# Tokens of the small blocks gathered and transposed ahead, and the second transposes' copies split, in an attention and mixture-of-experts kernel

## The chip, the cores and the metric

The kernel runs on one core of one Trainium2 chip. The metric is device time in microseconds (us) for one execution of the whole program, and lower is better. The core has a matmul engine (PE, with its weight loads shown as PEld), VectorE (DVE), ScalarE (ACT), GpSimd (POOL) and SyncE (SP, which here only issues DMAs). Each engine works through its own instructions in order and waits for others by semaphores.

## The reference: what is computed

Block-local attention with pooled far keys makes x of 3072 tokens by 512, and a two-level router sends each token to one of 16 experts. Cut to what matters here:

```python
x = attn_out.transpose(0, 2, 1, 3).reshape(B * S, H * D)      # 3072 x 512
for g in range(4):                                             # group of the token
    for e in range(4):                                         # expert within the group
        mask_e = ...                                           # tokens routed to expert (g, e)
        h = np.maximum(xg[mask_e] @ w1[g, e], 0.0)             # 512 -> 1024
        ye = h @ w2[g, e]                                      # 1024 -> 512
        out[tok_idx] = combined[:, None] * ye
```

How many tokens each expert gets depends on the data; the kernel counts them on the chip.

## The kernel before

The first part of the program is the attention (to about 175 us), with the router's arithmetic woven in. Then come the experts. Each expert's tokens are cut into blocks of 128: "first" blocks (four, of the largest expert), "pairs" (two blocks of one expert, 256 tokens), "ones" (single blocks left over) and "smalls" (a remainder of at most SM = 32 tokens, which would waste a whole block). The numbers of pairs, ones and smalls are read into registers, and `rest` (L1296) runs the blocks under `If`s: for i in 0 to BESIDE - 1 = 3 pair i and then small i, after that the other pairs, then the ones. With this data there are 8 pairs, 3 smalls and 3 ones, so smalls 0, 1 and 2 run behind pairs 0, 1 and 2.

A pair (`pair`, L1158) computes `stage1_2` (x times w1, with both split into a high and a low float32r part) and then twice `stage2` (h times w2), one for each half of 128 tokens. `stage2` is a generator: it hands back control after every 6 of its 24 matmuls, and there `pair` puts one part of `split_w`, which makes the next pair's high and low w1 (`w1h` by a cast on ACT, then `w1l` by a subtraction on DVE, 4 parts in all, in half 0 only). Each pair also starts the loads of the next pair's weights and, for i from 1 to 3, of small i's weights, on SP's queue.

A small (`small`, L1230) uses plain float32 and packs the 32 tokens four times into the 128 columns: the gather `gather_small` (L1226) brings one 128-column chunk of a token to each partition. Its steps follow each other on PE:

- a transpose of the gathered tokens into the PSUM tile `tp` (bank "tr" 2), and a copy of it by DVE into `xTs`;
- 16 matmul calls with w1 (stage 1), a Relu by ACT into `hs`;
- two transposes of `hs` into `tp`, a single DVE copy of both into `hTs`;
- 32 matmul calls with w2 (stage 2, chunks c = 0 to 7 in order), a scaled copy by ACT, and a scatter on POOL.

The gather of small i + 1 is issued in small i, behind its first transpose; that of small 0 in `first` (L1272). All of a small's buffers (`xgs`, `ys`, `xTs`, `hs`, `hTs`) are 128-column slices of one tile that the router no longer needs, so the profile shows them all as `eq_unit`. The operations made through `self.T` and `self.V` are all shown with line L123, a helper's. `bank` returns a fixed PSUM tile of one bank once the first blocks are done.

Of the kernel before, what the change touches and what calls it, by code (L numbers as in the profile page):

```python
# [20 lines left out]
P = 128  # L21
# [18 lines left out]
SM = 32  # L40
# [3 lines left out]
BESIDE = 4  # L44
SMALL = 2 * NPAIR + NONE
SLOTS = SMALL + NSM
KC, FC = DM // P, FF // P
# [28 lines left out]
class Banks:  # L76


    def __init__(self, tiles):
        self.tiles, self.n = tiles, 0  # L80
# [888 lines left out]
class Experts:  # L969
# [12 lines left out]
    def tiles(self, pool, early):  # L982
        def ring(name, shape, dt, n):
            return [pool.tile(shape, dt, name=f"{name}{j}") for j in range(n)]

        def pair(name, shape, n):
            return list(zip(ring(name + "h", shape, F32R, n), ring(name + "l", shape, F32R, n)))
        if early:
            self.w2r["first"] = self.w2r[1] = pool.tile([P, FC, DM], F32, name="w2r1")
            self.w1s = pair("w1", [P, KC, FC, P], 1)[0]  # L990

            self.xg1 = ring("xg", [P, DM], F32, 2)

            self.xT2 = ring("xT", [P, 2, KC, 2, P], F32R, 1)
            self.hT2 = pair("hT", [P, FC, 2 * P], 1)[0]

            o = self.router.ohr
            self.xT2.append(o[:, 0:16].rearrange("p (m c a) t -> p m c a t", m=2, a=2))
            self.xg2 = [None, o[:, 16:24].bitcast(F32).rearrange("p (a c) t -> p a (c t)", a=2)]
        else:  # L1000
            self.w1r[0], self.w1r[1] = ring("w1r", [P, KC, FF], F32, 2)
            self.w2r[0] = pool.tile([P, FC, DM], F32, name="w2r0")
            self.w2s = pair("w2", [P, FC, DM], 1)[0]
            self.xg2[0] = pool.tile([P, 2, DM], F32, name="xd")
            self.xT1 = ring("xs", [P, KC, P], F32, 2)
            self.y = ring("y", [P, DM], F32, 2)
            self.ny = 0
            eq = self.router.eq = pool.tile([P, NT, SLOTS], F32, name="eq_unit")
            parts = [eq.rearrange("p t s -> p (t s)")[:, P * i:P * i + P] for i in range(9)]
            self.xgs, self.ys, self.xTs = parts[0:2], parts[2:4], parts[4]  # L1010
            self.hs = eq.rearrange("p t s -> p (t s)")[:, 5 * P:7 * P]
            self.hTs = eq.rearrange("p t s -> p (t s)")[:, 7 * P:9 * P].rearrange("p (c r) -> p c r", r=SM)

# [144 lines left out]
    def pair(self, i):  # L1158

        row, nxt = ("unit", i), ("unit", i + 1)

        self.gather2(i + 2)
        self.load_w(("next", i + 1), 0)
        if 0 < i < BESIDE:
            self.load_w(("small", i), 0, self.n_small > i)
        for k, _ in enumerate(self.stage1_2(i)):
            if k % 2 == 0:
                self.split_w(row, 1, [k // 2])  # L1170
            if k == XT_AT:
                self.x_t2(i + 1)
        self.load_w(("next", i + 1), 1)
        if 0 < i < BESIDE:
            self.load_w(("small", i), 1, self.n_small > i)
        if i == 0:
            self.x_t_one(0)
        for half in range(2):
            hs = slice(half * P, half * P + P)
            for part, _ in enumerate(self.stage2([t[:, :, hs] for t in self.hT2], row, half, half)):  # L1180
                if half == 0 and i + 1 < NPAIR:
                    self.split_w(nxt, 0, [part])


    def gather_one(self, i):
# [39 lines left out]

    def gather_small(self, i):  # L1226
        if i < NSM:
            self.gather(("small", i), self.xgs[i % 2])

    def small(self, i):  # L1230

        nc, row = self.nc, ("small", i)
        w1, w2 = self.raw(row, 0), self.raw(row, 1)
        groups = [slice(SM * g, SM * g + SM) for g in range(P // SM)]
        tp = self.bank("tr", 2)
        self.T.transpose(out=tp[:, 0:P], in_=self.xgs[i % 2], identity=self.ident)
        self.gather_small(i + 1)
        self.V.tensor_copy(out=self.xTs, in_=tp[:, 0:P])
        bank = self.bank("lg", 0)
        hp, yp = bank[:, 0:2 * P], bank[:, 2 * P:3 * P]  # L1240

        def load(which):
            if i + 1 < NSM:
                more = self.n_small > i + 1
                self.load_w(("small", i + 1), which, more if i >= BESIDE - 1 else more * (self.n_pairs <= i + 1))
        for c in range(KC):
            for g, rows in enumerate(groups):
                self.T.matmul(out=hp[rows], lhsT=self.xTs[:, SM * c:SM * c + SM], rhs=w1[:, c, 2 * P * g:2 * P * g + 2 * P],
                              start=(c == 0), stop=(c == KC - 1), skip_group_check=True)
        nc.scalar.activation(out=self.hs, in_=hp, func=AF.Relu)  # L1250
        load(0)
        for m in range(2):
            self.T.transpose(out=tp[:, P * m + P:P * m + 2 * P], in_=self.hs[:, P * m:P * m + P], identity=self.ident)
        self.V.tensor_copy(out=self.hTs.rearrange("p (g m) r -> p m g r", m=2),
                           in_=tp[:, P:3 * P].rearrange("p (m g r) -> p m g r", m=2, r=SM))
        for c in range(FC):
            for g, rows in enumerate(groups):
                self.T.matmul(out=yp[rows], lhsT=self.hTs[:, c], rhs=w2[:, c, P * g:P * g + P],
                              start=(c == 0), stop=(c == FC - 1), skip_group_check=True)
        load(1)  # L1260
        y = self.ys[i % 2]
        nc.scalar.activation(out=y, in_=yp, func=AF.Copy, scale=self.tabs["small", "weight"][:, i:i + 1])
        self.put(y, row)
# [8 lines left out]
    def first(self):  # L1272
        for i in range(0, NE, 2):
            for k, _ in enumerate(self.stage1_2(0)):
                if i == 0 and k >= 4:
                    self.split_w(("first", 0), 1, [k - 4], what="h")
                yield
            if i + 2 < NE:
                self.x_t1()
                yield  # L1280
            for half in range(2):
                s2 = self.stage2([t[:, :, half * P:half * P + P] for t in self.hT2], ("first", i + half),
                                 late=None if i + half else lambda c: self.split_w(("first", 0), 1, [c], what="l"))
                if i + half < NE - 1:
                    yield from s2
        yield "units"
        for part, _ in enumerate(s2):
            self.split_w(("unit", 0), 0, [part])
            if part == 0:
                self.x_t2(0)  # L1290
                for i in range(2):
                    self.gather_one(i)
                self.gather_small(0)
        self.fixed = True

    def rest(self):  # L1296
# [49 lines left out]
def block_attention_then_moe(tc, q, k, v, w_group, w_expert, w1, w2, out):  # L1346
    with ExitStack() as st:
# [15 lines left out]
        def hook(n, need, space):  # L1363

            if not ex.w1r and n >= W1_AT and (router.ready & 1 or n == last - 4):
                need(1)
                ex.w1r["first"] = space
                ex.load_w(("first", 0), 0)
            if n == last - 4:
                ex.tiles(st.enter_context(tc.tile_pool(name="m_w", bufs=1, side="right")), True)  # L1370
            if n == last - GATHER_AT:
                need(2)
                ex.gather1(0)
            if n == last - W2_AT:

                ex.load_w(("first", 0), 1, queue=tc.nc.scalar)
            if n == last - X_AT:
                ex.x_t1()
                if NE > 2:
                    ex.gather1(2)  # L1380
            for part in range(4):
                if n == last + SPLIT_AT[part]:
                    ex.split_w(("first", 0), 0, [part])
            for _ in range(FIRST.get(n - last, 0)):
                next(first)
# [63 lines left out]
```

## Time and profile before

| | us |
|---|---|
| median of 3 runs | 541.56 |
| lowest and highest of them | 539.62, 542.04 |
| the profiled execution | 543.24 |
| its span, first to last instruction | 541.5 |

The profile comes from one execution. A row of the timeline gives the start from the beginning of the span, the duration, engine, line, operation, what is written and read, the count of merged instructions, and in brackets the idle time of the engine before it and what ended that. `PEclk` in the rows by windows is the granted clock of PE as a share: 1.00 is 2.4 GHz and 0.50 is 1.2 GHz.

### The profile page before, as it was taken

The numbers are of one execution on the slowest core, as the hardware profiler recorded it, in microseconds if no ns is written. First come the engines' busy times: TensorE is split into PE (matmuls) and PEld (weight loads), VectorE is DVE, ScalarE is ACT, GpSimd is POOL, SyncE is SP. The second block draws the span as 40 slices with busy tenths as digits, with TensorE's granted clock in tenths as the row PEclk, the third lists the DMA queues.
The fourth block names the chain that finished last, engine by engine and source line by source line (L and its number), as shares of the span: only waits on it lengthen the run. The fifth ranks groups of instructions, "written<-read, shape, count | busy, mean of one in ns | idle before, by whom it ended". The sixth has DMA issues, their size and how long they took to land. (4 is left out here: it accounts for less than half of the span.)

```text
span 541.5 us, 13168 instructions
## 1 busy us (share of the span) xinstructions
PE 492.9 (91%) x4873; PEld 412.7 (76%) x4873; DVE 312.2 (58%) x1001; ACT 289.0 (53%) x561; POOL 151.2 (28%) x166
## 2 busy tenths in 40 slices
PE   6798888898989899989979899999999999999991
PEld 3576667677777787979859697889898998977770
DVE  6666788788865869756706354465474836540000
ACT  5688888899976551116615354445464644541110
POOL 6553543353443201054021130402021121210110
PEclk9899999999987999988989999999999999999997
DMA  9668965796681620299719879667666657636950
GB/s 225 141 152 160 210 175 143 176 209 149 143 274 41 234 79 21 77 385 399 289 37 374 321 292 391 217 207 259 231 198 232 213 197 245 244 105 242 305 194 21
DMA packets 80837, 111.15 MB, mean 205 GB/s; under 512 B 42732, under 2 KB 51310, under 8 KB 77936
## 3 DMA queue, kind: packets, MB, share of 16 engines
q1 hardware_dynamic: 74992, 93.31, 55.5%
q0 software_dynamic: 4704, 14.69, 7.4%
q10 hardware_dynamic: 1056, 2.10, 1.1%
q8 instruction: 44, 0.72, 0.6%
q14 instruction: 41, 0.34, 0.2%
HBM read 118.27 MB, written 13.04 MB: 242 GB/s over the span
## 5 line engine op out<-in xcount | busy, mean ns | idle before, releaser
L123 PE MATMUL ps_s<-xT,w1h 128*128 128x256 f32 x448 | 84.2, 285 | 0.4 <-PEq L1328 0.4
L123 DVE TENSOR_TENSOR w2l<-w2r,w2h 128x1024 fp32r<-128x1024 f32 x40 | 48.8, 1226 | 53.8 <-ACT w2h L1064 51.9
L1116 POOL DMA_INDIRECT out_dram<-y,t_unit_scatter x21 | 22.1, 1050 | 193.7 <-ACT y L1110 106.3
L123 PEld LDWEIGHTS ps_s<-xT,w1h 128*128 128x128 f32 x448 | 70.7, 191 | 1.6 <-issue 1.3
L123 PE MATMUL ps_s<-xT,w1l 128*128 128x256 f32 x224 | 63.3, 283 | 0.0
L821 ACT ACTIVATE pr<-ss,nm 128x120 f32<-128x120 f32 x192 | 60.1, 388 | 3.9 <-DVE nm L812 3.5
L1154 ACT ACTIVATE hTh<-ps_s 128x512 fp32r<-128x512 f32 x44 | 26.3, 598 | 55.6 <-PE ps_s L123 35.1
L750 POOL TENSOR_TENSOR va<-vr,share 24x512 f32<-24x512 f32 x48 | 49.6, 1058 | 14.4 <-DMA vr<-vs 11.0
L123 DVE TENSOR_TENSOR w1l<-w1r,w1h 128x1024 fp32r<-128x1024 f32 x40 | 46.5, 1222 | 3.0 <-ACT w1h L1064 3.0
L123 PE MATMUL ps_s<-ohr,w1h 128*128 128x256 f32 x256 | 48.1, 286 | 0.0
L123 DVE SCALAR_TENSOR_TENSOR hTl<-ps_s,hTh 128x512 fp32r<-128x512 f32 x44 | 30.4, 690 | 27.7 <-ACT hTh L1154 27.7
L812 DVE CUSTOM_DVE_ANT_0 ss<-mask,ps_s 128x120 f32<-128x120 f32 x192 | 42.0, 274 | 3.0 <-ACT pr L821 2.3
L123 PEld LDWEIGHTS ps_s<-xT,w1l 128*128 128x128 f32 x224 | 42.8, 191 | 0.2
L1064 ACT CAST w2h<-w2r 128x1024 fp32r<-128x1024 f32 x40 | 41.5, 1042 | 0.8 <-issue 0.4
L123 PEld LDWEIGHTS ps_s<-ohr,w1h 128*128 128x128 f32 x256 | 40.5, 192 | 0.7 <-issue 0.6
L829 ACT COPY ptS<-ps_tr 121x512 f32<-121x512 f32 x48 | 28.1, 586 | 20.3 <-PE ps_tr L123 8.2
L1064 ACT CAST w1h<-w1r 128x1024 fp32r<-128x1024 f32 x40 | 38.9, 1046 | 0.0
L123 PE MATMUL ps_s<-kw,qt 64*64 64x120 f32 x768 | 34.1, 284 | 4.6 <-DVE kw L757 2.3
L790 POOL COPY kw<-kf 128x1152 f32<-128x1152 f32 x15 | 17.3, 1154 | 73.5 <-DVE kf L781 39.4
L777 ACT ACTIVATE qt<-ps_tr 64x384 f32<-64x384 f32 x64 | 33.3, 521 | 5.9 <-PE ps_tr L123 4.7
L123 PE MATMUL ps_s<-ohr,w1l 128*128 128x256 f32 x128 | 36.3, 284 | 0.0
L123 PE MATMUL ps_s<-w2h,hTh 128*128 128x512 f32 x88 | 35.7, 406 | 0.0
(255 smaller groups left out, 1050.2 us busy)
## 6 DMA issues: line engine op xcount, KB each, us to landing
w1r<-in_moe_w_dram SPq DMA_DIRECT2D x40, 1024.0 KB
w2r<-in_moe_w_dram SPq DMA_DIRECT2D x40, 1024.0 KB
va<-in_v_dram SPq DMA_DIRECT2D x32, 240.0 KB
kn<-in_k_dram SPq DMA_DIRECT2D x16, 384.0 KB
qn<-in_q_dram SPq DMA_DIRECT2D x16, 384.0 KB
x_dram<-xt SPq DMA_DIRECT2D x12, 512.0 KB
w_first<-in_moe_w_dram SPq DMA_DIRECT2D x2, 1024.0 KB
w2r<-in_moe_w_dram ACTq DMA_DIRECT2D x2, 1024.0 KB
```

The costliest lines, as they stand in the source:

```text
L123: return f(*args, **kw)
L750: nc.gpsimd.tensor_tensor(out=va_ring[idx % NVA][KW:NC, t:t + n, :, 0:D], in0=vr[KW:NC].broadcast_to([NBLK, n, 2, D]), in1=by(share, KW, N ...
L777: nc.scalar.activation(out=by_run(qb, h)[:, j], in_=tv, func=AF.Copy, scale=-1.0 / 8.0)
L790: (nc.gpsimd if idx else V).tensor_copy(out=kw[:, :, 0:KW], in_=tiles)
L812: V.tensor_tensor_reduce(out=ss[:, u], in0=mask[:, 1 if t == 0 else 2 if t == NQT - 2 else 0], in1=sp[h][:, j], scale=1.0, scalar=3.4e38, ...
L821: nc.scalar.activation(out=pr[:, i, 0:NC], in_=sp[:, i], func=AF.Exp, bias=nm[:, i:i + 1], scale=-1.0)
L829: nc.scalar.copy(out=ptS.rearrange("p a c -> p (a c)"), in_=pt[0:NR])
L1064: self.nc.scalar.copy(out=h, in_=src)
L1116: self.nc.gpsimd.indirect_dma_start(out=out, out_offset=bass.IndirectOffsetOnAxis(ap=self.tabs[name, "scatter"][:, col:col + 1], axis=0), ...
L1154: nc.scalar.activation(out=th[:, js], in_=hp, func=AF.Relu)
```

## The change

Three things are changed. First, the tokens of smalls 0 to 3 are all gathered in `first`, one behind the other on POOL, into four buffers (two of them in slices that later hold `hs` and `hTs`). Second, their transposes and DVE copies (`x_t_small`) move from the smalls into pair 0: two of them behind the third part (18 matmuls) of `stage2` for half 0, and two at the same place for half 1; all four go through bank "tr" 2. Smalls 4 and later keep the old way. Third, behind the Relu of a small, the two transposes get a copy each: the first's is made by ACT, the second's by DVE, and stage 2 takes the chunks in the order 0, 2, 4, 6, 1, 3, 5, 7, so that its first half needs ACT's copy only.

```diff
-            parts = [eq.rearrange("p t s -> p (t s)")[:, P * i:P * i + P] for i in range(9)]
-            self.xgs, self.ys, self.xTs = parts[0:2], parts[2:4], parts[4]
+            parts = [eq.rearrange("p t s -> p (t s)")[:, P * i:P * i + P] for i in range(8 + BESIDE)]
+            self.xgs, self.ys, self.xTs = parts[0:2] + parts[5:8:2], parts[2:4], parts[4:5] + parts[9:8 + BESIDE]
...
                 if half == 0 and i + 1 < NPAIR:
                     self.split_w(nxt, 0, [part])
+                if i == 0 and part == 2:
+                    for j in range(2 * half, min(2 * half + 2, BESIDE)):
+                        self.x_t_small(j)
...
+    def x_t_small(self, i):
+        tp = self.bank("tr", 2)[:, i % 2 * P:i % 2 * P + P]
+        self.T.transpose(out=tp, in_=self.x_in(i), identity=self.ident)
+        self.V.tensor_copy(out=self.x_small(i), in_=tp)
...
     def small(self, i):
+        if i >= BESIDE:
+            self.x_t_small(i)
+        if i >= BESIDE - 1:
+            self.gather_small(i + 1)
+        xT = self.x_small(i)
         tp = self.bank("tr", 2)
-        self.T.transpose(out=tp[:, 0:P], in_=self.xgs[i % 2], identity=self.ident)
-        self.gather_small(i + 1)
-        self.V.tensor_copy(out=self.xTs, in_=tp[:, 0:P])
...
-        for m in range(2):
-            self.T.transpose(out=tp[:, P * m + P:P * m + 2 * P], in_=self.hs[:, P * m:P * m + P], identity=self.ident)
-        self.V.tensor_copy(out=self.hTs.rearrange("p (g m) r -> p m g r", m=2),
-                           in_=tp[:, P:3 * P].rearrange("p (m g r) -> p m g r", m=2, r=SM))
-        for c in range(FC):
+        hTs = self.hTs.rearrange("p (g m) r -> p m g r", m=2)
+        for m, copy in enumerate((nc.scalar.copy, self.V.tensor_copy)):
+            tm = tp[:, P * m + P:P * m + 2 * P]
+            self.T.transpose(out=tm, in_=self.hs[:, P * m:P * m + P], identity=self.ident)
+            copy(out=hTs[:, m], in_=tm.rearrange("p (g r) -> p g r", r=SM))
+        order = [*range(0, FC, 2), *range(1, FC, 2)]
+        for c in order:
...
-                self.gather_small(0)
+                for i in range(BESIDE):
+                    self.gather_small(i)
```

## Rows read from the trace of the kernel before

**Rows 1.** The page's first section: busy us (share of span) x instructions, by engine.

```profile
PE 492.9 (91%) x4873; PEld 412.7 (76%) x4873; DVE 312.2 (58%) x1001; ACT 289.0 (53%) x561; POOL 151.2 (28%) x166
```

**Rows 2.** Windows: length; busy of PE, PEld, DVE, ACT, POOL; PEclk, DMA share, GB/s.

```profile
284.30:306.60 22.30, 22.30 (x144) 20.25 (x144) 13.14 (x14) 10.74 (x14) 3.58 (x3) 1.00 1.01 380
...
309.50:311.00 1.50, 0.44 (x3) 0.20 (x3) 0.42 (x1) 0.38 (x1) 1.20 (x2) 1.00 0.04 14
```

**Rows 3.** Timeline of small 1, all engines (small 2 repeats it within 0.01 us).

```profile
306.85 0.27 PE L123 MATMUL ps_tr<-ident,eq_unit 128*128 128x128 f32 x1
...
307.16 0.29 DVE L123 COPY eq_unit<-ps_tr 128x128 f32<-128x128 f32 x1 [5.06 <-PE ps_tr L123]
...
307.55 1.93 PE L123 MATMUL ps_lg<-w1r,eq_unit 128*32 128x256 f32 x32 [0.43 <-issue]
...
309.61 0.38 ACT L1250 ACTIVATE eq_unit<-ps_lg 128x256 f32<-128x256 f32 x1 [1.82 <-PE ps_lg L123]
310.04 0.44 PE L123 MATMUL ps_tr<-ident,eq_unit 128*128 128x128 f32 x2 [0.56 <-ACT eq_unit L1250]
310.52 0.42 DVE L123 COPY eq_unit<-ps_tr 128x256 f32<-128x256 f32 x1 [3.06 <-PE ps_tr L123]
...
311.00 2.10 PE L123 MATMUL ps_lg<-w2r,eq_unit 128*32 128x128 f32 x64 [0.52 <-DVE eq_unit L123]
```

**Rows 4.** Timeline of small 0: the same first step on PE.

```profile
274.39 0.27 PE L123 MATMUL ps_tr<-ident,eq_unit 128*128 128x128 f32 x1
275.05 1.94 PE L123 MATMUL ps_lg<-w1r,eq_unit 128*32 128x256 f32 x32 [0.38 <-DVE eq_unit L123]
```

**Rows 5.** Groups with shapes kept apart: 128x128 moves out of PSUM, busy, mean ns.

```profile
L1262 ACT ACTIVATE eq_unit<-ps_lg,t_small_weight 128x128 f32<-128x128 f32 x3 | 1.1, 368 | 10.2 <-PE ps_lg L123 10.2
L123 DVE COPY eq_unit<-ps_tr 128x128 f32<-128x128 f32 x3 | 0.9, 292 | 15.2 <-PE ps_tr L123 15.2
```

**Rows 6.** Timeline in the attention: two engines empty one PSUM tile (L781).

```profile
42.38 0.50 ACT L781 COPY kf<-ps_tr 64x384 f32<-64x384 f32 x1
...
42.91 0.56 DVE L781 COPY kf<-ps_tr 64x384 f32<-64x384 f32 x1 [0.80 <-ACT kf L781]
```

**Rows 7.** Timeline of pair 0's stage 2: DVE's subtractions and PE at the two places.

```profile
266.17 2.36 DVE L123 TENSOR_TENSOR w1l<-w1r,w1h 128x1024 fp32r<-128x1024 f32 x2
268.44 1.22 DVE L123 TENSOR_TENSOR w1l<-w1r,w1h 128x1024 fp32r<-128x1024 f32 x1
...
267.42 0.40 PE L123 MATMUL ps_av<-w2h,hTh 128*128 128x512 f32 x1
...
273.00 0.39 PE L123 MATMUL ps_s<-w2h,hTh 128*128 128x512 f32 x1
```

**Rows 8.** Timeline of PE: four transposes and the first matmul behind them.

```profile
262.74 0.65 PE L123 MATMUL ps_tr<-ident,xg 128*128 128x128 f32 x4
263.15 0.48 PE L123 MATMUL ps_av<-w2h,hTh 128*128 128x512 f32 x1
```

**Rows 9.** Timeline of POOL around small 0's gather; DMA issues with us to landing.

```profile
244.49 1.00 POOL L1072 DMA_INDIRECT eq_unit<-x_dram,t_small_gather  x1 [0.30 <-issue]
251.48 1.02 POOL L1116 DMA_INDIRECT out_dram<-y,t_first_scatter  x1 [5.99 <-ACT y L1110]
...
eq_unit<-x_dram,t_small_gather POOLq DMA_INDIRECT x1, 6.1
```

**Rows 10.** Windows of half a microsecond around small 1: length, PEclk, DMA share, GB/s.

```profile
309.50:310.00 0.50, 1.00 0.04 16
310.00:310.50 0.50, 1.00 0.00 0
```

**Rows 11.** Small 0: ACT's Relu in the timeline, and two windows (columns of rows 2).

```profile
278.43 0.38 ACT L1250 ACTIVATE eq_unit<-ps_lg 128x256 f32<-128x256 f32 x1 [3.15 <-PE ps_lg L123]
...
277.50:280.90 3.40, 1.51 (x42) 1.28 (x46) 0.42 (x1) 0.38 (x1) 0.41 (x1) 1.00 0.11 35
280.90:284.30 3.40, 3.40 (x41) 3.01 (x33) 0.36 (x1) 1.35 (x2) 1.01 (x1) 0.50 0.00 0
```

More of the change, by code (lines that the diff above doesn't have):

```diff
@@ L1227, in gather_small, with x_in, x_small @@
         if i < NSM:
-            self.gather(("small", i), self.xgs[i % 2])
+            self.gather(("small", i), self.x_in(i))
+    def x_in(self, i):
+        return self.xgs[i if i < BESIDE else i % 2]
+    def x_small(self, i):
+        return self.xTs[i if i < BESIDE else 0]
+    def x_t_small(self, i):
+        tp = self.bank("tr", 2)[:, i % 2 * P:i % 2 * P + P]
+        self.T.transpose(out=tp, in_=self.x_in(i), identity=self.ident)
+        self.V.tensor_copy(out=self.x_small(i), in_=tp)
     def small(self, i):
@@ L1247, in small @@
             for g, rows in enumerate(groups):
-                self.T.matmul(out=hp[rows], lhsT=self.xTs[:, SM * c:SM * c + SM], rhs=w1[:, c, 2 * P * g:2 * P * g + 2 * P],
+                self.T.matmul(out=hp[rows], lhsT=xT[:, SM * c:SM * c + SM], rhs=w1[:, c, 2 * P * g:2 * P * g + 2 * P],
                               start=(c == 0), stop=(c == KC - 1), skip_group_check=True)
@@ L1251, in small @@
         load(0)
-        for m in range(2):
-            self.T.transpose(out=tp[:, P * m + P:P * m + 2 * P], in_=self.hs[:, P * m:P * m + P], identity=self.ident)
-        self.V.tensor_copy(out=self.hTs.rearrange("p (g m) r -> p m g r", m=2),
-                           in_=tp[:, P:3 * P].rearrange("p (m g r) -> p m g r", m=2, r=SM))
-        for c in range(FC):
+        hTs = self.hTs.rearrange("p (g m) r -> p m g r", m=2)
[5 more added lines that the diff above has]
+        for c in order:
             for g, rows in enumerate(groups):
                 self.T.matmul(out=yp[rows], lhsT=self.hTs[:, c], rhs=w2[:, c, P * g:P * g + P],
-                              start=(c == 0), stop=(c == FC - 1), skip_group_check=True)
+                              start=(c == order[0]), stop=(c == order[-1]), skip_group_check=True)
         load(1)
```

## The prediction

> **What bounds the kernel now.** I read the page's busy times first: PE is busy for 91% of the span, and no other engine comes near it [rows 1]. Then I read the windows around a small block. In the pair between smalls 0 and 1 PE is busy in all of 22.30 us; in 1.5 us inside small 1 it is busy for 0.44 [rows 2]. So in this part PE sets the time, a pair leaves nothing to gain, and a small holds PE's idle time in two places. The timeline shows them. The first is the token transpose: it starts at 306.85, DVE copies from 307.16 to 307.45, and stage 1 starts at 307.55, so PE spends 0.70 us on a step that itself needs about 0.1 [rows 3, 8]. The second lies behind the Relu: transposes at 310.04, DVE's copy at 310.52, stage 2 at 311.00, which is 0.96 us. Whatever is removed there comes off the end of the program, as PE's later work all queues behind it; whatever is put into pair 0's stage 2 on PE is added one for one.
>
> **What is removed.** Without the token step the first matmul of stage 1 can start where the transpose started. That is 0.70 us in smalls 1 and 2 [rows 3] and 0.66 in small 0 [rows 4]: 2.06 us. The three gathers that leave the smalls were beside PE's work and give nothing.
>
> **What is added on POOL.** Three more gathers stand behind the one at 244.49, each 1.00 us and 0.30 of issue, so POOL is done at about 249.4. Queued behind them is the scatter that begins at 251.48 because it waits for ACT [rows 9], then pair 0's token gathers. Cost nothing, with 2 us of cover; without that cover they would delay the scatter by 3.9 us, for which PE doesn't wait. They land some 6 us after issue [rows 9], at about 256, and PE wants the first at 267.42.
>
> **What is added in pair 0.** This is the step on which the sum turns. The two transposes of one half write different columns of one PSUM bank, and each is followed by a DVE copy out of it. If the second transpose may start at once, each costs PE its own 0.10 us (four and the switch back took 0.41, [rows 8]) and nothing else. If engines take turns on a bank, the second waits for the first's copy, and PE, which works in order, holds all of stage 2 behind it. The trace has no such transpose. The nearest row is in the attention: ACT and DVE each copy one half of the partitions of one PSUM tile, no data ties them, and DVE starts at 42.91, 0.03 us after ACT's end at 42.88, after 0.80 us of waiting that is put down to ACT [rows 6]. I take it that accesses to one bank are put in order also when their regions differ. (The two also write interleaved columns of one SBUF tile, so that could be the reason; hence a chance for the other reading, below.)
>
> The Trainium skill's page "PSUM — Partial Sum Buffer", section "PSUM bank collisions raise a hardware error", says that the compiler back end adds a dependency between any two instructions of different engines that touch the same bank and 32-partition quadrant, whatever the address. [rows 6] agree, and go further, as the partitions differ too. By that rule the sum is the one of the forecast; without it, that of the second rival.
>
> With taking turns, half 0: PE reaches the place at 267.42. DVE's copy stands in its queue behind the third subtraction, so it can start when the fourth did, at 268.44 [rows 7]. It takes 0.29 [rows 5], and PE follows a DVE copy by 0.10 (307.45 to 307.55, [rows 3]): 268.83. The second transpose adds 0.10. PE goes on at 268.93 instead of 267.42: 1.51 us. Half 1: at 273.00 DVE has no subtraction left (the fourth ends at 269.66, [rows 7], and 0.6 later in the changed kernel), so the step costs what it did in a small, 0.70, and 0.10 for the second transpose: 0.80. Together 2.3 us. The bounds are 0.4 (all four at 0.10) and 2.8 (0.23 more for each pair of transposes if the switch of operand kind is dear); I take 2.3, from the nearest rows. The fourth subtraction is late by 0.6 us; its reader is pair 1, which stands behind small 0, whose Relu alone is at 278.43 [rows 11], so that is hidden by over 8 us.
>
> **The split copy.** Before, stage 2 follows the first transpose by 0.96 us. Taking turns, the chain is: first transpose 0.27; PE to ACT 0.13 (309.48 to 309.61); ACT's copy 0.37 (the nearest row is ACT's own 128x128 move; DVE's 0.29 is the low end, [rows 5]); ACT to PE 0.05 (309.99 to 310.04); second transpose 0.17, about half of the 0.44 less its tail [rows 3]: 0.99 us. So the second transpose, which now stands behind ACT's copy, eats the gain: +0.03 each, between -0.05 and +0.05, for three smalls +0.1. Without turns the second transpose runs beside ACT, and the chain is 0.82: -0.14 each. DVE's copy of the second half is ready about 1.5 us after the first transpose; the odd chunks are wanted at 0.99 plus half of 2.10, that is 2.04 [rows 3]: hidden by 0.5 us, which is what it would cost uncovered.
>
> **The new order of chunks** wants the second half of w2 after two chunks instead of four, 0.52 us earlier, in a small that is 0.70 earlier anyway. In small 1 that moves the need from 312.05 (311.00 plus 1.05) to 310.83; the load's last bytes move before 310.0 [rows 10]. Loads start with the pair, so they move along. Cost nothing, with some 0.5 us of slack.
>
> **Sum.** -2.06 + 2.3 + 0.1 = +0.35 us, between -0.1 and +1.0 with the bounds of the turn-taking case. The profiled execution took 543.24 (span 541.5 and 1.7 around it), so it would be 543.6; it lies 1.7 above the median of the runs, 541.56. On that median the forecast is 541.9.
>
> **Rivals.**
> - Small 0 loses its extra time. There the Relu starts at 278.43, though stage 1's last matmul is modelled to end at 276.99 [rows 4, 11]; in small 1 that step takes 0.13 us, so 1.3 us are lost to something the profile doesn't name. After this stretch, in which PE was busy for 1.51 of 3.40 us, the granted clock stood at 0.50 (1.2 GHz) for 3.40 us of full work [rows 11], which loses half of it, 1.7. If the earlier start of stage 1 or the gather's absence removes both, 3.0 us go: 538.9. For it: smalls 1 and 2 have neither. Against it: nothing shows that the removed step caused them, and the median run may not have had them.
> - The bank does not make engines take turns, so the change does all that it says: -2.06 + 0.4 - 0.4 = -2.1, that is 539.5. Against it stand [rows 6].
> - Slower: the half clock comes to pair 0. The 1.4 us in which PE stands at 267.5, on top of the 0.6 at 273.1 and small 0's own gaps, could be followed by a granted clock of 0.50, as the gaps of small 0 were [rows 11]. Each such stretch of 3.40 us costs 1.7; two of them give 541.9 + 3.4 = 545.3. [...] Against it: smalls 1 and 2 have gaps of 0.4 to 0.6 us with no fall, and pair 0 is dense before and after its gap.
>
> **How the numbers follow.** Forecast 0.58, small 0's loss gone 0.20, no turns 0.13, slower 0.09. The range 538.8 to 543.9 holds the forecast with its bounds and the spread of the runs, and reaches to the first two rivals; it leaves out the slower one and the cases in which both gains come together. A measurement of this kernel can tell about 0.5%, 2.7 us, from no change. Faster than 538.85 needs the first rival in full, or two gains at once: 0.11. Slower than 544.27 is the third rival: 0.09. Within: 0.80.
>
> **What would show it.** In the changed profile: stage 1 of each small starts right behind the pair's last matmul, with no DVE copy before it. In pair 0 PE waits for a DVE copy of `eq_unit` twice, 1.3 to 1.4 us in half 0, ended by DVE behind the third subtraction, and 0.4 to 0.6 in half 1. In a small the second transpose starts after ACT's copy, and stage 2 still starts 0.9 to 1.0 us after the first. I am wrong if the two transposes of a half stand 0.1 us apart, if the Relu of small 0 follows its matmuls at once, or if stage 2 waits for a DMA.

## The result

The changed kernel took 542.46 us (median of 20 executions, 539.37 to 546.82) where the kernel before took 539.52 beside it (median of 20, 537.27 to 542.12). The ratio is 1.0056, with an interval of 1.0032 to 1.0080, that is +3.0 us (+1.7 to +4.3). The forecast was +0.35 on a median of 541.56, 541.9, with a range of 538.8 to 543.9. So the time lies in the range, and the change sits about at the bound of what I called no change (0.5%, 2.7 us); its size was missed by some 2.7 us.

The page's first line of the changed kernel stands beside [rows 1]; its profiled execution took 542.27 with a span of 540.5.

```profile
PE 494.3 (91%) x4874; PEld 413.1 (76%) x4874; DVE 312.4 (58%) x1002; ACT 290.5 (54%) x564; POOL 148.4 (27%) x166
```

Nothing is to be seen in it: the same engine is busy for the same share. The timeline of pair 0 tells more. These rows of the changed kernel (ACT, DVE, then PE) answer [rows 7]:

```profile
265.65 3.89 ACT L1064 CAST w1h<-w1r 128x1024 fp32r<-128x1024 f32 x4 [0.41 <-DMA w1r<-in_moe_w_dram]
...
266.73 3.50 DVE L123 TENSOR_TENSOR w1l<-w1r,w1h 128x1024 fp32r<-128x1024 f32 x3 [1.24 <-ACT w1h L1064]
270.14 0.28 DVE L123 COPY eq_unit<-ps_tr 128x128 f32<-128x128 f32 x1
270.85 0.29 DVE L123 COPY eq_unit<-ps_tr 128x128 f32<-128x128 f32 x1 [0.42 <-PE ps_tr L123]
271.06 1.22 DVE L123 TENSOR_TENSOR w1l<-w1r,w1h 128x1024 fp32r<-128x1024 f32 x1
...
268.64 0.27 PE L123 MATMUL ps_tr<-ident,eq_unit 128*128 128x128 f32 x1
270.48 0.33 PE L123 MATMUL ps_tr<-ident,eq_unit 128*128 128x128 f32 x1 [1.57 <-DVE eq_unit L123]
276.23 0.27 PE L123 MATMUL ps_tr<-ident,eq_unit 128*128 128x128 f32 x1
276.88 0.33 PE L123 MATMUL ps_tr<-ident,eq_unit 128*128 128x128 f32 x1 [0.39 <-DVE eq_unit L123]
```

The first transpose of half 0 is at 268.64, the second only at 270.48, right behind DVE's copy at 270.14, and that stands behind the third subtraction. Stage 2 goes on at 270.57, 1.93 us after the first transpose. In half 1 the same step takes 0.74 (276.23 to 276.97). The first row is new: the chain does not begin at DVE. DVE's subtractions wait for ACT's cast of w1, and that for the landing of the next pair's w1 (0.41 us). In the kernel before nothing on PE hung on this chain until pair 1.

The next rows are small 0 and small 1, to be read beside [rows 3, 4]:

```profile
278.54 1.93 PE L123 MATMUL ps_lg<-w1r,eq_unit 128*32 128x256 f32 x32
280.54 0.38 ACT L1266 ACTIVATE eq_unit<-ps_lg 128x256 f32<-128x256 f32 x1 [1.21 <-PE ps_lg L123]
280.98 0.33 PE L123 MATMUL ps_tr<-ident,eq_unit 128*128 128x128 f32 x1 [0.50 <-ACT eq_unit L1266]
281.34 0.27 ACT L1272 COPY eq_unit<-ps_tr 128x128 f32<-128x128 f32 x1 [0.42 <-PE ps_tr L123]
281.66 0.33 PE L123 MATMUL ps_tr<-ident,eq_unit 128*128 128x128 f32 x1 [0.35 <-ACT eq_unit L1272]
281.92 1.95 PE L123 MATMUL ps_lg<-w2r,eq_unit 128*32 128x128 f32 x64
...
307.49 1.93 PE L123 MATMUL ps_lg<-w1r,eq_unit 128*32 128x256 f32 x32
...
310.92 2.17 PE L123 MATMUL ps_lg<-w2r,eq_unit 128*32 128x128 f32 x64
...
311.57 1.25 PEld L123 LDWEIGHTS ps_lg<-w2r,eq_unit 128*32 128x32 f32 x48 [0.27 <-DMA w2r<-in_moe_w_dram]
```

Stage 1 follows the pair with no DVE copy in between. The second transpose follows ACT's copy (0.35 of idle time, ended by ACT), and stage 2 starts 0.94 after the first transpose, where it was 0.96 [rows 3]. In small 1 the weights of stage 2 wait 0.27 for a DMA. And small 0's Relu comes 0.07 behind its matmuls, not 1.4 as in [rows 11]; the windows of small 0 hold no half clock either (columns as in [rows 2]):

```profile
278.50:281.90 3.40, 2.54 (x35) 1.21 (x34) 0.00 (x0) 1.34 (x3) 1.01 (x1) 1.00 0.11 43
281.90:285.30 3.40, 3.40 (x77) 3.18 (x77) 0.29 (x1) 1.36 (x2) 0.71 (x1) 1.00 0.02 5
```

So two of the three things by which I said I would be wrong are there: small 0's Relu is on time, and a stage 2 waits for a DMA. The two transposes of a half didn't stand 0.1 apart: the second was held until DVE had copied the first out of the bank, which is the forecast's case of taking turns.

### The profile page after: what moved, and what is told of

It is laid out like the page before. It is cut to its first block, busy times and chain, and to the rows that moved or that the text cites. A ratio compares the mean times of both kernels' runs of the same rounds, so it can differ in the third digit from the quotient of the medians.

```text
span 540.5 us, 13183 instructions
## 1 busy us (share of the span) xinstructions
PE 494.3 (91%) x4874; PEld 413.1 (76%) x4874; DVE 312.4 (58%) x1002; ACT 290.5 (54%) x564; POOL 148.4 (27%) x166
```

## The experiments

All ratios are to the kernel before, run beside the kernel on the same chip. The groups of runs came to different chips, and the kernel before took 539.5 (first comparison), 543.94 (e0 to e3), 538.95 (e5 to e8), 544.06 (e9, e11, e12; the chip of e0 to e3 again) and 543.11 us (e10, another chip again); which chip the first comparison ran on is not on record. The chip turned out to matter.

To compare traces I cut the span from the start of pair 0's stage 2 to the end into stretches, by the starts of PE's rows: A, pair 0's stage 2 up to stage 1 of small 0; B, on to pair 1; C, on to stage 1 of small 1; D, on to pair 2; E, on to stage 1 of small 2; F, on to pair 3; G, the rest. What comes before stage 2 is left out.

| us | A | B | C | D | E | F | G | sum |
|---|---|---|---|---|---|---|---|---|
| before (profiled) | 11.90 | 7.39 | 25.11 | 5.48 | 24.44 | 5.59 | 198.45 | 278.36 |
| e3 (before, gathers ahead) | 11.90 | 5.28 | 24.29 | 5.33 | 24.43 | 5.33 | 198.33 | 274.89 |
| e6 (before, w1 later) | 11.90 | 5.28 | 24.28 | 5.33 | 24.44 | 5.32 | 198.31 | 274.85 |
| after (profiled) | 14.17 | 5.27 | 23.68 | 5.53 | 23.82 | 5.39 | 198.31 | 276.17 |
| e7 (after again) | 13.66 | 5.26 | 23.69 | 5.73 | 23.82 | 5.42 | 198.24 | 275.82 |
| e1 (two banks) | 11.79 | 5.72 | 23.66 | 5.97 | 23.83 | 5.72 | 198.45 | 275.14 |
| e10 (all in half 1) | 12.99 | 5.70 | 23.69 | 5.90 | 23.82 | 5.72 | 198.44 | 276.26 |
| e8 (two banks, new order) | 11.79 | 5.29 | 23.68 | 5.33 | 23.83 | 5.33 | 198.39 | 273.64 |

**Two banks for the transposes (e1).** Theory 1 is the forecast's: engines take turns on a PSUM bank, and so PE stands behind DVE in pair 0.

```diff
-        tp = self.bank("tr", 2)[:, i % 2 * P:i % 2 * P + P]
+        tp = self.bank("tr", i % 2 if i < BESIDE else 2)[:, 0:P]
```

> The changed kernel, but the two transposes of a half write two different PSUM banks ("tr" 0 and 1, both idle in pair 0's stage 2), so no transpose shares a bank with the copy before it. Theory 1, the loss is PE standing in pair 0 for a DVE copy out of the same bank: the 1.85 us and 0.66 us between the two transposes of a half shrink to 0.1 to 0.3, and with 2.06 us saved in the smalls the time is 1 to 2 us below the kernel before, ratio 0.996 to 0.998. Theory 2, the three gathers moved ahead delay the loads: the time stays 2 to 3 us above, ratio 1.004 to 1.006. Theory 3, the split copy costs in the smalls: the same, 1.004 to 1.006.

Measured: 540.18 us, ratio 0.9943 (0.9922 to 0.9964). It is below the 0.996 to 0.998 expected, because the kernel before loses some 3 us in small 0 on this chip that e1 doesn't (e3, below). PE's timeline in pair 0, then in small 1:

```profile
267.78 0.38 PE L123 MATMUL ps_tr<-ident,eq_unit 128*128 128x128 f32 x2
273.60 0.38 PE L123 MATMUL ps_tr<-ident,eq_unit 128*128 128x128 f32 x2
...
308.11 0.64 PE L123 MATMUL ps_lg<-w2r,eq_unit 128*32 128x128 f32 x16
309.21 1.52 PE L123 MATMUL ps_lg<-w2r,eq_unit 128*32 128x128 f32 x48 [0.45 <-DMA w2r<-in_moe_w_dram]
```

The two transposes of a half merge into one row (x2), and stretch A falls from 14.17 to 11.79. Only the place of the transposes in PSUM was changed, so the stand in pair 0 was the turn on the bank. (Each bank is one tile of the program here, so an order by bank and one by tile can't be told apart.) The second pair of rows shows what the early start met: after two chunks (16 of 64 matmuls) stage 2 of small 1 waits for the second half of w2. Stretches D and F are 0.6 and 0.4 longer than in e3; the wait is all of the first, but only some 0.1 of the second, and for the rest of it the profile names no DMA.

**The split copy alone (e2).** Kernel before, with ACT's and DVE's copies and the new order, nothing else (the third part of the change):

```diff
-        for m in range(2):
-            self.T.transpose(out=tp[:, P * m + P:P * m + 2 * P], in_=self.hs[:, P * m:P * m + P], identity=self.ident)
-        self.V.tensor_copy(out=self.hTs.rearrange("p (g m) r -> p m g r", m=2),
-                           in_=tp[:, P:3 * P].rearrange("p (m g r) -> p m g r", m=2, r=SM))
+        for m, copy in enumerate((nc.scalar.copy, self.V.tensor_copy)):
...
+        order = [*range(0, FC, 2), *range(1, FC, 2)]
```

> The kernel before with the split copy and the new chunk order alone. Theory 1: the second transpose behind ACT's copy eats what the shorter copy gives, -0.03 us in each small, ratio 1.000. Theory 3: above 1.003.

Measured: 542.67 us, ratio 0.9997 (0.9977 to 1.0017). It is worth nothing, as forecast.

**The gathers alone (e3), and the kernel before once more (e0).** In e3 four gathers stand in `first`, into four buffers of their own; transposes and copies stay in the smalls.

```diff
-            self.gather(("small", i), self.xgs[i % 2])
+            self.gather(("small", i), self.xgs[i % 4])
...
-        self.gather_small(i + 1)
+        if i >= BESIDE - 1:
+            self.gather_small(i + 1)
...
-                self.gather_small(0)
+                for i in range(BESIDE):
+                    self.gather_small(i)
```

> The kernel before with the four gathers ahead alone (into buffers of their own), the transposes still in the smalls. Theory 1: 192 KB more in the stretch where the loads are dense put the landing of the next w1 off by about 0.5 us, which nobody on PE waits for, ratio 1.000. Theory 2: above 1.003.

> The kernel before once more, for a second trace of it. If the late Relu of small 0 and the half clock behind it (3.0 us together) were chance, small 0 here takes about 6.2 us from its first transpose to pair 1, as smalls 1 and 2 do; if they belong to the kernel, 8.0 us again.

Measured: e3 540.24 us, ratio 0.9939 (0.9918 to 0.9959); e0 542.0 (one execution). e3 was to give nothing and gave 3.3 us. The table shows where: B falls from 7.39 to 5.28 and C from 25.11 to 24.29, 2.9 us, which is the late Relu and the half clock of [rows 11]. In e0's trace both are there again (its stage 1 at 273.93, pair 1 at 282.11, B = 8.18). So moving the gathers is not the neutral part that I took it for.

**Only the gather of small 1 moved (e9), and the kernel before again (e11).** e9 issues one gather more in `first` and none in small 0; smalls 1 and 2 keep theirs.

```diff
-        self.gather_small(i + 1)
+        if i >= 1:
+            self.gather_small(i + 1)
...
-                self.gather_small(0)
+                for i in range(2):
+                    self.gather_small(i)
```

> The kernel before, in which only the gather of small 1 is issued ahead (behind that of small 0, into the second of the two buffers), so that no gather is issued in small 0; the gathers of smalls 2 and 3 stay in smalls 1 and 2. Theory 2 (small 0's loss hangs on a gather issued in it, and appears only where the kernel before takes 541.5 or more): ratio 0.993 to 0.996 there, with small 0 at 5.9 us from its first transpose to pair 1, and 0.999 to 1.001 where the kernel before takes under 541. Rival (the loss is that of the first small, whatever it issues): 1.000 in both, with the same late Relu.

> The kernel before, unchanged, one look, beside the two runs of this group on one chip. Small 0 lost about 3 us in three traces of one kind (first transpose to the next pair's first matmul 8.0 to 8.8 us, with stage 1's end seen 1.4 us late and a granted clock of 0.50 after it), but not in the trace with the extra load (5.9 us), which ran where the kernel before took 538.95 us and not 543.94. Theory 2 (whether small 0 loses them depends on the chip or the execution, not on the program): the loss is here if the time is 541.5 to 545, and not if it is 537 to 541. Rival (the extra load moved something and that took the loss away): the loss is here whatever the time.

Measured: e9 540.76 us, ratio 0.9928 (0.9906 to 0.9950), with e11 at 543.84 beside it. Timeline of e11 in small 0:

```profile
277.43 1.05 POOL L1072 DMA_INDIRECT eq_unit<-x_dram,t_small_gather  x1 [0.30 <-issue]
278.98 0.38 ACT L1250 ACTIVATE eq_unit<-ps_lg 128x256 f32<-128x256 f32 x1 [3.15 <-PE ps_lg L123]
```

and of e9 at the same place (stage 1 at 276.94, in e11 at 275.60):

```profile
278.94 0.38 ACT L1251 ACTIVATE eq_unit<-ps_lg 128x256 f32<-128x256 f32 x1 [1.77 <-PE ps_lg L123]
```

The Relu comes 3.38 us after the start of stage 1 with a gather issued beside it, and 2.00 without. What follows is in e11's windows, first the stretch with the wait, then the one after it:

```profile
277.15:280.55 3.40, 1.00 (x18) 0.38 (x14) 0.43 (x1) 0.38 (x1) 1.05 (x1) 1.00 0.19 67
281.00:284.40 3.40, 3.40 (x55) 3.02 (x45) 0.00 (x0) 0.85 (x2) 0.20 (x1) 0.50 0.00 0
```

After PE was busy for 1.00 of 3.40 us the granted clock is 0.50, which is 1.2 GHz. So the one gather in small 0 costs 1.4 us of waiting and then the half clock: the loss I had left as a rival whose cause "the profile doesn't name" belongs to that gather. Smalls 1 and 2 issue a gather too, but at another place. In e11 small 0's starts at 277.43, 0.1 before the modelled end of stage 1 (275.60 plus 1.93), and small 1's 1.3 behind it, beside stage 2:

```profile
311.40 1.05 POOL L1072 DMA_INDIRECT eq_unit<-x_dram,t_small_gather  x1 [0.30 <-PE ps_tr L123]
311.58 2.17 PE L123 MATMUL ps_lg<-w2r,eq_unit 128*32 128x128 f32 x64 [0.52 <-DVE eq_unit L123]
```

There it costs less: with such a gather stage 2 of smalls 1 and 2 takes 2.02 to 2.33 (first profile, e0, e2, e9, e11), and without one 1.95 (e3). What in the gather holds PE stays open.

**The load of w1 later (e5, e6).** Pair 0 loads the next pair's w1 twice, in the changed kernel (e5) and in the kernel before (e6).

```diff
+        if i == 0:
+            self.load_w(("next", 1), 0)
```

> The changed kernel, in which pair 0 first loads the next pair's w1 once more (2 MB extra, about 5.5 us at the 380 GB/s of a pair), so that the w1 that is split lands that much later. Theory 1: TensorE's stand in half 0 grows by the same 4 to 5.5 us and the program by about that, less what the next pairs take back; ratio to the time before 1.006 to 1.012. Rival (the stand is one turn of VectorE and isn't tied to the load): the stand stays at 1.5 to 2 us and the ratio within 0.003 of the changed kernel's, apart from what the same extra load costs the kernel before.

> The kernel before with the same extra 2 MB load in pair 0. Here nothing on TensorE waits behind the subtractions of half 0 until pair 1. Theory 1: 1.000 to 1.003; the subtractions end about 5.5 us later, which pair 1, some 12 us behind them, doesn't see; at most the loads behind it (w1 and w2 of small 1 and of the next pair) come late once by a part of it. Rival (every load behind is late by 5.5 us and TensorE waits for one of them): 1.006 to 1.010, and then the growth of the changed kernel under the same load is no evidence.

Measured: e5 547.37 us, ratio 1.0149 (1.0116 to 1.0182), more than the 1.006 to 1.012 expected; e6 538.57 us, ratio 0.9996 (0.9973 to 1.0018). The timeline of e5 in pair 0:

```profile
269.10 3.88 ACT L1064 CAST w1h<-w1r 128x1024 fp32r<-128x1024 f32 x4 [4.94 <-DMA w1r<-in_moe_w_dram]
...
273.59 0.28 DVE L123 COPY eq_unit<-ps_tr 128x128 f32<-128x128 f32 x1
...
267.56 0.27 PE L123 MATMUL ps_tr<-ident,eq_unit 128*128 128x128 f32 x1
273.93 0.48 PE L123 MATMUL ps_tr<-ident,eq_unit 128*128 128x128 f32 x1 [6.10 <-DVE eq_unit L123]
```

and its windows behind that stand:

```profile
273.90:277.30 3.40, 3.37 (x10) 2.71 (x11) 1.42 (x2) 0.25 (x1) 0.00 (x0) 0.56 0.02 7
277.30:279.00 1.70, 1.70 (x9) 1.38 (x8) 0.00 (x0) 0.44 (x1) 0.98 (x1) 1.00 0.00 0
```

The cast waits 4.94 for the load and PE 6.10 for DVE. In e6 the cast waits about as long (4.70 for the same load), and the program takes no longer. So the change has tied PE to the landing of a load that had over 10 us to spare (in [rows 7] the subtractions are done 6.5 us after stage 2 began, and in e6 pair 1 begins 17.2 after it). The third rival is here too: behind a stand of 6.5 us the granted clock is 0.56 for 3.4 us of work, which costs another 1.3 us or so. Stretch A is 20.05, against 13.66 in e7 on the same chip: 5.08 from the stand (6.50 for 1.42), the rest with the clock.

**All four transposes in half 1 (e10).** There DVE has no subtraction in its queue; the bank stays shared.

```diff
-                if i == 0 and part == 2:
-                    for j in range(2 * half, min(2 * half + 2, BESIDE)):
+                if i == 0 and half == 1 and part in (1, 2):
+                    for j in range(2 * part - 2, 2 * part):
```

> The changed kernel, in which all four transposes of tokens stand in half 1 of pair 0 (two behind the second part, two behind the third), where VectorE has no subtraction in front of them; they still share one bank. Theory 1 (each pair of transposes on one bank costs one turn of VectorE, 0.74 us, and half 0 cost more only because VectorE stood behind the cast and the load of w1): no stand in half 0, two of 0.7 to 0.8 us in half 1, 1.5 us in all where the changed kernel has 2.7; 0.9 to 1.2 us less than the changed kernel, that is 0.995 to 0.998 of the time before where that is over 541.5 us and 1.000 to 1.003 where it is under 541. Rival (the stand follows the transposes wherever they go, since TensorE waits for more than VectorE's turn): stands of 1.5 us or more in half 1 and the time of the changed kernel.

Measured: 540.57 us, ratio 0.9966 (0.9942 to 0.9990), beside 543.11 before. PE's timeline:

```profile
270.16 0.27 PE L123 MATMUL ps_tr<-ident,eq_unit 128*128 128x128 f32 x1
270.81 0.33 PE L123 MATMUL ps_tr<-ident,eq_unit 128*128 128x128 f32 x1 [0.38 <-DVE eq_unit L123]
272.38 0.27 PE L123 MATMUL ps_tr<-ident,eq_unit 128*128 128x128 f32 x1
273.03 0.33 PE L123 MATMUL ps_tr<-ident,eq_unit 128*128 128x128 f32 x1 [0.38 <-DVE eq_unit L123]
```

Two turns, each 0.74 from the first transpose to stage 2 going on (270.90, 273.12), and A is 12.99, 1.18 below the changed kernel's. So a bare turn costs 0.74, and the other 1.2 of half 0 came from the queue in front of DVE's copy. It lost 0.4 in small 0 and 0.6 and 0.4 in D and F, as e1 did. D's is the wait for w2 (0.65 on PEld in small 1), small 0's is taken up under e8, and in F no wait for a DMA stands.

**The changed kernel again (e7), and a version with the two banks and another order of chunks (e8).** e8 is e1 with

```diff
-        order = [*range(0, FC, 2), *range(1, FC, 2)]
+        order = [0, 2, 1, 3, 4, 6, 5, 7]
```

> The changed kernel unchanged, on the same chip as the runs that stand beside it. Theory 1 (the stand of TensorE in half 0 of pair 0 lasts until VectorE has come through three subtractions that wait for ScalarE's cast, and that for the landing of the next pair's w1): 0.998 to 1.004 of the time before, with the first transpose of half 0 put down to VectorE, and the second transpose 1.5 to 4 us behind the place at which the sixth chunk of stage 2 ended; how long depends on when the load of w1 lands in that execution. Small 0 runs with a granted clock of 1.00 and without the late Relu. Rival (the extra time beyond the forecast is a granted clock of 0.50 somewhere in pair 0 or before it): a stretch at 0.50 behind 262 in the windows of the slower executions, with the stand at 1.5 to 2 us.

> The changed kernel with two edits: the four transposes of tokens write two PSUM banks in turn (as in the run with two banks), and stage 2 of a small takes the chunks in the order 0, 2, 1, 3, 4, 6, 5, 7, so that the second half of w2 is wanted after four chunks and no longer after two. Theory 1: no turn to wait for in pair 0, and stage 2 of smalls 1 and 2 no longer waits for the landing of w2's second half (0.45 us in small 1 with two banks alone): 0.991 to 0.995 of the time before, 0 to 0.9 us less than with two banks alone. Rival (the loads set the pace of smalls 1 and 2 anyway): the same time as with two banks alone, and a wait for a DMA of w2r still there or moved to pair 2.

Measured: e7 541.57 us, ratio 1.0029 (1.0010 to 1.0049); e8 539.49 us, ratio 0.9992 (0.9971 to 1.0013). In e7's pair 0 w1 landed in time:

```profile
265.83 3.89 ACT L1064 CAST w1h<-w1r 128x1024 fp32r<-128x1024 f32 x4
266.92 3.50 DVE L123 TENSOR_TENSOR w1l<-w1r,w1h 128x1024 fp32r<-128x1024 f32 x3 [0.73 <-ACT w1h L1064]
269.34 0.27 PE L123 MATMUL ps_tr<-ident,eq_unit 128*128 128x128 f32 x1
270.33 0.28 DVE L123 COPY eq_unit<-ps_tr 128x128 f32<-128x128 f32 x1
270.67 0.33 PE L123 MATMUL ps_tr<-ident,eq_unit 128*128 128x128 f32 x1 [1.06 <-DVE eq_unit L123]
```

No DMA stands in the brackets of the cast, and the step takes 1.42 (269.34 to 270.76), where 1.51 was forecast and the first profile had 1.93. (Between the two transposes lie 1.33, a little under the 1.5 to 4 expected.) In e8 D and F are 5.33 as in e3: with the second half of w2 wanted after four chunks, stage 2 doesn't wait. Its trace has the smallest sum of all, 1.25 below e3, but by time it can't be told from the kernel before on this chip, which took 538.95; 0.991 to 0.995 was expected.

So on this chip there was little to win back. e6, the kernel before but for a load, ran there, and its small 0 has no late Relu (B = 5.28). That alone doesn't show what the unchanged kernel does there, for the load put the gather off, from stage 1 to stage 2 of small 0 (e6):

```profile
273.96 1.93 PE L123 MATMUL ps_lg<-w1r,eq_unit 128*32 128x256 f32 x32 [0.38 <-DVE eq_unit L123]
...
277.36 1.96 PE L123 MATMUL ps_lg<-w2r,eq_unit 128*32 128x128 f32 x64 [0.52 <-DVE eq_unit L123]
278.11 1.05 POOL L1072 DMA_INDIRECT eq_unit<-x_dram,t_small_gather  x1 [0.30 <-issue]
```

But this gather costs stage 2 nothing, in any of e6's three smalls (1.95 to 1.96), where those in e0, e2, e9 and e11 do. And the versions with the gathers ahead show the same for a scatter on POOL, which all of them issue 1.07 or 1.08 us after the start of small 0's stage 1. In e1, with stage 1 at 275.30:

```profile
276.38 1.01 POOL L1116 DMA_INDIRECT out_dram<-y,t_unit_scatter  x1 [4.74 <-ACT y L1110]
277.75 0.38 ACT L1266 ACTIVATE eq_unit<-ps_lg 128x256 f32<-128x256 f32 x1 [1.65 <-PE ps_lg L123]
```

and in e8, whose program is the same up to there, with stage 1 at 273.63:

```profile
274.71 1.01 POOL L1116 DMA_INDIRECT out_dram<-y,t_unit_scatter  x1 [4.40 <-ACT y L1110]
275.63 0.38 ACT L1266 ACTIVATE eq_unit<-ps_lg 128x256 f32<-128x256 f32 x1 [1.21 <-PE ps_lg L123]
```

The Relu comes 2.45 us after the start of stage 1 in e1 and 2.00 in e8. It is 2.44 in e10 and e12, where the kernel before took 543 to 544, and 2.00 in the changed kernel, e5 and e7, where it took 539.0 to 539.5. So the same program has its Relu on time on some chips and late on others. That it is the scatter that makes it late is argued from e9's gather; no run leaves the scatter out.

**A bank for each transpose of the small as well (e12).** e8, and

```diff
-            tm = tp[:, P * m + P:P * m + 2 * P]
+            tm = self.bank("tr", m)[:, 0:P]
```

> The run with two banks and the order 0, 2, 1, 3, 4, 6, 5, 7, in which also the two transposes behind a small's Relu write a bank each. Theory 1 (two engines take turns on a bank, so that the second transpose waits for ScalarE's copy of the first): the second transpose now follows the first by 0.1 to 0.2 us where it was 0.68, and stage 2 follows the first by 0.78 to 0.86 where it was 0.94; 0.1 to 0.15 us for each of three smalls, 0.4 in all, too small to be told apart by its time from the run with two banks; 0.991 to 0.995 of the time before where that is over 541.5, 0.997 to 1.000 where it is under 541. Rival (the second transpose waits for something else, its weights or the switch to float32): it stays 0.6 to 0.7 behind the first.

Measured: 540.05 us, ratio 0.9917 (0.9898 to 0.9936), beside 544.06 before. Timeline of small 1:

```profile
309.19 0.44 PE L123 MATMUL ps_tr<-ident,eq_unit 128*128 128x128 f32 x2 [0.55 <-ACT eq_unit L1265]
...
309.88 0.81 PEld L123 LDWEIGHTS ps_lg<-w2r,eq_unit 128*32 128x32 f32 x32 [0.48 <-ACT eq_unit L1271]
309.88 2.52 PE L123 MATMUL ps_lg<-w2r,eq_unit 128*32 128x128 f32 x64 [0.25 <-ACT eq_unit L1271]
...
310.94 0.58 PEld L123 LDWEIGHTS ps_lg<-w2r,eq_unit 128*32 128x32 f32 x20 [0.25 <-DMA w2r<-in_moe_w_dram]
```

The second transpose no longer waits for ACT's copy, and stage 2 follows the first by 0.69 where it was 0.94. Stage 2 then takes 2.52 in place of 1.95, so small 1 ends no earlier: a wait of 0.25 for w2 stands in it, and further on one of 0.24 for which the profile names nothing, while a scatter on POOL has just ended.

## Why the forecast held, and what it missed

**The time** came within 0.6 us of the forecast partly by luck. The base, 541.56, was the median of three executions and 2.0 above the 539.52 measured beside the changed kernel, and the change was 2.7 larger than the +0.35 of the sum; the two errors nearly cancel.

**The turn on the bank** was right, and it was the step on which the sum turned. The changed kernel shows it twice, e1 and e12 take it away by a bank alone, e10 prices it at 0.74. The rule of the Trainium skill's page "PSUM — Partial Sum Buffer", section "PSUM bank collisions raise a hardware error", that the compiler back end adds a dependency between two engines' instructions on a bank and partition quadrant whatever the address, agrees with all four: two transposes into disjoint columns of one bank held stage 2 for 1.93 us in half 0, into two banks for 0.14 (267.78 to 267.92 in e1). Its other half, that different quadrants may run side by side, was tried in no run here. [rows 6], which the prediction took for support, are of that other half, as their partitions differ; what held DVE there stays open.

**Half 0** was forecast at 1.51. It measured 1.42 in e7 and 1.93 in the first profile. The mechanism was right, the term was read off one execution: in [rows 7] the subtractions had their w1 in time. What I hadn't named is that ACT's cast and the landing of w1 stand in front of DVE's copy, so the term has no upper bound of its own; e5 put it at 6.50. My bound of 2.8 for both halves covered the switch of operands and left out the load. (At the low end the prediction's -0.1 doesn't follow from its terms, which give +0.1.)

**Half 1** was forecast at 0.80 and measured 0.74. **The split copy**: forecast +0.03 each; the chain measured 0.94 instead of 0.96, since ACT's copy took 0.27 and not 0.37. e2 confirms that it gives nothing.

**The three gathers on POOL** were to cost nothing in front, and do: from POOL's first `t_unit_gather` to stage 2 of pair 0 it is 28.7 us in e0 (233.31 to 262.03) and in e3 (234.91 to 263.62). The cover was not there in e3, since two of the three gathers take 1.9 to 2.0 us each and the scatter stands behind them until 254.29, but PE doesn't wait for it. (The traces in which the 28.7 are 29.7 to 30.0 are of both kinds: the first profiles of both kernels, e6 and e8.)

**The removed token step** was taken at 2.06. C and E fell by 0.61 each against e3, not 0.70: a transpose started 0.24 behind the pair's last matmul (276.05 to 276.29 in e9), stage 1 starts 0.33 behind it (278.21 to 278.54). **Entering and leaving the transposes** cost some 0.2 more that the sum didn't have: in e8, where they take 0.27 in all, A falls by 0.11 and not by 0.34 (0.61 - 0.27).

**The new order of chunks** was costed at nothing, with some 0.5 us of slack (0.8 by its own 310.83 and 310.0). That step failed. The slack was read in small 1 of the profile, whose pair 1 was 0.8 longer by the half clock (C, 25.11 for 24.29), while the load doesn't slow with it: it is there at most 27.6 us after the start of pair 1 in that profile (282.44 to 310.0) and 27.8 in the changed kernel, where stage 2 waits for it (283.81 to 311.57). In the changed kernel the second half of w2 is wanted 0.6 plus 0.5 earlier, and the wait is 0.27 in small 1; in e1, 0.45. D and F together are 0.26 and 0.49 above e3 in the two traces of the changed kernel and 1.03 in e1, some 0.3 of it not w2's; e8, which only puts the order back in halves, has neither.

Added up against e3: A +2.27, B and G -0.03, C and E -1.22, D and F +0.26, which is +1.28 us in the first profile; e7 gives +0.93. That is the forecast's +0.35 with its mis-sized terms.

**Small 0's loss** was the first rival, and its mechanism is real: in e3 the three gathers ahead take away 2.9 us. I had called the gathers' part neutral ("beside PE's work and give nothing"), which failed in e3 and e9. That the rival still didn't give the result has one reading that fits all runs: on the chips where the kernel before took 539.0 to 539.5 its small 0 doesn't lose the 3 us, on those where it took 543 to 544 it does. The profile before, at 543.24, is of the second kind and 1.7 above its runs' median, which I had noted as a doubt. The traces show the loss in all four that have the gather beside stage 1 (the first profile, e0, e2, e11), and a Relu late beside the same scatter on the chips of the second kind alone (e1, e10 and e12 against the changed kernel, e5, e7 and e8). e6, without the loss, takes what the kernel before takes beside it (0.9996, where 3 us less would be 0.9944). But no trace of the unchanged kernel from a chip of the first kind was taken, so that its gather costs nothing there is argued, not shown; nor do the traces give all of the difference between the chips (sums of 278.2 to 278.3 in e0 and e11 and 274.85 in e6, 3.4 of 5 us). The changed kernel itself wasn't run on the other chips. From e10's 0.9966, with the 0.7 to 1.2 us that its A is shorter than the changed kernel's, I would estimate 0.998 to 0.999 there.

**What stays open.** The traces give +0.9 to +1.3 against a kernel before without the loss (e3, and e6 within 0.1 of it); the ratios give +1.6 (e7) and +3.0 (first comparison). The stretch before pair 0's stage 2, which the table leaves out, can't settle it: it lasts 261.8 us in e8 and 265.1 in e7, on one chip, and the two programs differ only behind it. The changed kernel's executions spread over 7.5 us (539.37 to 546.82), those before over 4.9. e5 shows what a later w1 does, with the half clock behind it, and that would make such a spread; no trace of one of the long executions exists to show that it was this.

## What to carry to other kernels

Before a small step is moved into a dense stretch, write down which engine it will wait for and then everything that stands in front of that engine's part, down to the loads: a wait of 0.7 us became 1.4 to 1.9 here, and 6.5 with a late load. Two tiles that different engines work on in turn want a PSUM bank each; that alone was worth 1.9 to 2.4 us in pair 0 (A, 13.66 or 14.17 to 11.79). A loss that the profile shows at a single place should be tried out by itself before the change is priced: moving one gather gave 0.7% on a chip that had the loss (e9), where the whole change with two banks gave no more (0.6%, e1). And a ratio from one chip needn't hold on another: e8 and e12 took 539.5 and 540.05 us, and their ratios are 0.9992 and 0.9917.

## What was not expected of the hardware

A gather issued on POOL beside a small's stage 1 went with a Relu 1.4 us late and then a granted clock of 0.50 for 3.4 us. With a scatter there the Relu was 0.4 us late on the chips where the kernel before took 543 to 544 us, and not at all on those where it took 539.0 to 539.5. The kernel before differed by 5 us between chips (538.95 and 544.06), more than any edit here gained, while the versions with two banks took 539.5 to 540.2 on both.
